# Tile 0 of the tokens in two column pieces, another load order, another order of the first W1 units, and the statistics of two tiles moved behind copies

## The chip, the cores and the metric

The kernel runs on one core of one Trainium2 chip. The metric is the device time of one execution in microseconds (us). A profile's "span" is the time from the first to the last instruction of the program in that one profiled execution; it is about 2 us less than the time of the same run. Engines: PE is the tensor engine, PEld its weight loads, DVE the vector engine, ACT the scalar engine, POOL the gpsimd engine, SP the engine that issues most loads.

Ratios are those of fast runs of one kernel over fast runs of the other in the same rounds, so they are not quite the ratio of the medians that are quoted beside them.

## The reference, cut to what matters

```python
xn = layernorm(x)                                   # x: 2048 tokens, 640 columns
out = x + attention(xn, wqkv, wo)                   # linear attention, 32 heads
        + gelu(xn @ w1 + b1) @ w2 + b2              # w1: 640 x 1536
```

The first matmul stage is `xn @ w1`. Before it a tile of 128 tokens has to be loaded, normalised, transposed (by PE) and copied from PSUM (the memory that PE's results go to) to SBUF (the memory that the next matmuls read). After all of W1 come the K stage (the matmuls for the keys) and, later, the q stage (those for the queries).

## The kernel before: the parts that matter

A helper records every instruction for an engine, and makes it wait for the writers of what it reads and the readers of what it overwrites. Each engine runs its own list in the order of the recording. The loads stand in one queue, issued by SP in this order:

```python
dma_x(0, 1)                                          # x tile 0
dma_w("sync", b1tmp[:], ..., r_b1tmp)                # bias, 3 KB
dma_w1(0)                                            # first quarter of W1: 384 of 1536 columns
dma_x(1, 1)
dma_w1(1)
dma_x(2, 1)
dma_w1(2)
dma_x(3, 1)
dma_w1(3)
# ... larger loads of x and the other weights follow
```

The helpers of one tile `t`:

```python
def ln_half(t, h):   # DVE: statistics of half of tile t's columns (needs x of the tile)
def ln_aggr(t):      # DVE: mean and variance; then two POOL instructions: rstd = 1 / sqrt(variance + eps)
def ln_norm(t):      # DVE: xn = (x - mean) * rstd, 640 columns
def transp(t):       # PE: five 128x128 transposes into a PSUM bank
def xnT_copy(t, b):  # DVE: PSUM -> SBUF, 640 columns
def b1_step():       # PE: transpose of the bias; ACT: copy of it
def h_unit(t0, n, jb):  # PE: 5 matmuls of n tiles with 128 columns of W1; ACT: gelu
```

The start and the order of the units, shortened: checks that a tile exists and the calls of `run_masks` (POOL work for a later stage) are left out (JT = 12 units of a tile, JQ = 3 units in each quarter of W1; `now` is the estimate of PE's time, in us):

```python
filler(11)                     # matmuls on zeros
ln_stats(0); ln_norm(0)
tb = transp(0)
b1_step()
filler(1)
ln_half(1, 0)
xnT_copy(0, tb)
ln_half(1, 1)
ln_aggr(1); ln_half(2, 0); ln_norm(1); ln_half(2, 1); ln_aggr(2)

plan = []
for q in range(2):
    plan += [(0, 1, jb) for jb in range(q * JQ, (q + 1) * JQ)]   # tile 0, quarters 0 and 1
for q in range(2):
    plan += [(1, 1, jb) for jb in range(q * JQ, (q + 1) * JQ)]   # tile 1, quarters 0 and 1
plan += [(0, 2, jb) for jb in range(2 * JQ, JT)]                 # both tiles, quarters 2 and 3
# ... then tile 2, tile 3, pairs, fours
now, nxt = 0.0, 1
for (t0, n, jb) in plan:
    while nxt < NT and (nxt < t0 + n or now >= 1.7 + 2.45 * (nxt - 1)):
        tb = transp(nxt)
        ln_half(nxt + 2, 0)        # statistics of a later tile ...
        xnT_copy(nxt, tb)          # ... ahead of the copy of this one
        ln_norm(nxt + 1)
        ln_half(nxt + 2, 1); ln_aggr(nxt + 2)
        nxt += 1; now += 0.3
    h_unit(t0, n, jb)
    now += 0.285 * n
```

Of the kernel before, what the change touches and what calls it, by code (L numbers as in the profile page):

```python
# [5 lines left out]
ALU = AluOpType  # L6
ACT = mybir.ActivationFunctionType
P = 128
FP32 = mybir.dt.float32
BF16 = mybir.dt.bfloat16  # L10
# [102 lines left out]
def bass_parallel_sum__linear_attn_block__dense_activation_gelu__prompt_kernel(  # L113
    nc: bass.Bass, A_x, A_wqkv, A_wo, B_x, B_w1, B_b1, B_w2, B_b2, out):
    Batch, S, D = A_x.shape
    F = B_w1.shape[1]
    assert Batch == 1 and D == 640 and F % P == 0 and S % 512 == 0
    NT = S // P
# [3 lines left out]
    DT = D // P  # L122
    JT = F // P
# [6 lines left out]
    Pl = Planner(nc)  # L130
    R_ = Pl.res
# [5 lines left out]
    with contextlib.ExitStack() as es:  # L137
# [3 lines left out]
        x_in = xPK  # L141
        PK = xPK
        xn_tm = sb("xn_tm", [P, NT, D], BF16)
        xnTf = sb("xnT", [P, DT * S], BF16)
        xnT = xnTf[:].rearrange("p (k s) -> p k s", k=DT)
        x_res = xnTf[:].rearrange("p (t d) -> p t d", t=NT)
        PQ = sb("PQ", [P, DT, S], BF16)
        HG = sb("HG", [P, JT, S], BF16)
        W1f = sb("W1", [P, DT * F], BF16)
        W1 = W1f[:].rearrange("p (k f) -> p k f", k=DT)  # L150
# [9 lines left out]
        b1tmp = sb("b1tmp", [JT, P], BF16)  # L160
        b1c = sb("b1c", [P, JT], FP32)
        b2bc = sb("b2bc", [P, D], BF16)
        ident = sb("ident", [P, P], BF16)
# [6 lines left out]
        aggr = sb("aggr", [P, 4, 2], FP32)  # L170
        veps = sb("veps", [P, 4], FP32)
        rstd = sb("rstd", [P, 4], FP32)
# [8 lines left out]
        B_ = [R_("bank%d" % i) for i in range(8)]  # L181
        ring = [0]

        def take(n):
            b = ring[0]
            if n == 2 and b % 2:
                b += 1
            b %= 8
            ring[0] = (b + n) % 8
            return b  # L190

        def bank(b, lo=0, hi=512):
            return ps[:, b * 512 + lo: b * 512 + hi]
# [7 lines left out]
        r_x = [R_("x%d" % t) for t in range(NT)]  # L201
        r_xr = [R_("xr%d" % c) for c in range(NC)]
        r_xb = [R_("xb%d" % t) for t in range(NT)]
        r_xn = [R_("xn%d" % t) for t in range(NT)]
        r_xnT = [R_("xnT%d" % t) for t in range(NT)]
        NW1 = 4
        r_W1 = [R_("W1_%d" % i) for i in range(NW1)]
        r_Wq, r_Wk, r_Wv, r_W2, r_Wo = R_("Wq"), R_("Wk"), R_("Wv"), R_("W2"), R_("Wo")
        r_b1tmp, r_b1c, r_b2 = R_("b1tmp"), R_("b1c"), R_("b2")
        r_ident, r_small, r_masks, r_bmask, r_warm = R_("ident"), R_("small"), R_("masks"), R_("bmask"), R_("warm")  # L210
        r_stats = [R_("stats%d" % i) for i in range(4)]
        r_aggr = [R_("aggr%d" % i) for i in range(4)]
        r_veps = [R_("veps%d" % i) for i in range(4)]
        r_rstd = [R_("rstd%d" % i) for i in range(4)]
# [3 lines left out]
        r_HG = [[R_("HG%d_%d" % (t, j)) for j in range(JT)] for t in range(NT)]  # L218
# [10 lines left out]
        def dma_x(t, n):  # L229
            src = xv[t * P:(t + n) * P, :].rearrange("(t p) d -> p t d", p=P)  # L230
            Pl.ins("sync", lambda e: e.dma_start(x_in[:, t:t + n, :], src),  # L231
                   writes=r_x[t:t + n], dma=True)

        def dma_w(eng, dst, src, res):
            Pl.ins(eng, lambda e: e.dma_start(dst, src), writes=[res], dma=True)  # L235
# [3 lines left out]
        FW = F // NW1  # L239
        def dma_w1(i):  # L240
            dma_w("sync", W1[:, :, i * FW:(i + 1) * FW], w1v[:, :, i * FW:(i + 1) * FW], r_W1[i])
        dma_x(0, 1)
        dma_w("sync", b1tmp[:], B_b1.rearrange("(a p) -> a p", p=P), r_b1tmp)
        dma_w1(0)
        dma_x(1, 1)
        dma_w1(1)
        dma_x(2, 1)
        dma_w1(2)
# [2 lines left out]
        for c in range(1, NC):  # L251
# [9 lines left out]
        v = "vector"  # L261
# [7 lines left out]
               reads=[r_ident], writes=[r_ident])  # L269
# [17 lines left out]
        def run_masks(n):  # L287
            for _ in range(min(n, len(mask_jobs))):
                mask_jobs.pop(0)()


        def filler(n):
            b = take(1)
            Pl.ins("tensor", [lambda e: e.matmul(bank(b), warm[:, 0:P], warm[:], start=True, stop=True)
                              for _ in range(n)], reads=[r_warm], writes=[B_[b]])

        def b1_step():
            b = take(1)
            Pl.ins("tensor", lambda e: e.transpose(bank(b).bitcast(BF16)[:, 0:JT], b1tmp[:], ident[:JT, :JT]),
                   reads=[r_b1tmp, r_ident], writes=[B_[b]])  # L300
            Pl.ins("scalar", lambda e: e.activation(b1c[:], bank(b).bitcast(BF16)[:, 0:JT], ACT.Copy),
                   reads=[B_[b]], writes=[r_b1c])


        def ln_half(t, h):
            s = t % 4
            Pl.ins(v, lambda e: e.bn_stats(stats[:, s, 6 * h:6 * h + 6], x_in[:, t, h * HW:(h + 1) * HW]),  # L307
                   reads=[r_x[t]], writes=[r_stats[s]])

        def ln_aggr(t):  # L310
            s = t % 4
            Pl.ins(v, lambda e: e.bn_aggr(aggr[:, s, :], stats[:, s, :]),
                   reads=[r_stats[s]], writes=[r_aggr[s]])
            Pl.ins(g, lambda e: e.tensor_single_scalar(veps[:, s:s + 1], aggr[:, s, 1:2], EPS, ALU.add),
                   reads=[r_aggr[s]], writes=[r_veps[s]])
            Pl.ins(g, lambda e: e.tensor_tensor(out=rstd[:, s:s + 1], in0=veps[:, s:s + 1],
                                                in1=mhalf[:], op=ALU.pow),
                   reads=[r_veps[s], r_small], writes=[r_rstd[s]])

        def ln_stats(t):  # L320
            ln_half(t, 0)
            ln_half(t, 1)
            ln_aggr(t)

        def ln_norm(t):
            s = t % 4
            Pl.ins(v, lambda e: e.tensor_scalar(xn_tm[:, t, :], x_in[:, t, :], aggr[:, s, 0:1], rstd[:, s:s + 1],
                                                ALU.subtract, ALU.mult),
                   reads=[r_x[t], r_aggr[s], r_rstd[s]], writes=[r_xn[t]])

        def transp(t):
            b = take(1)
            pT = bank(b).bitcast(BF16)[:, 0:D]
            Pl.ins("tensor", [(lambda e, k=k: e.transpose(pT[:, k * P:(k + 1) * P],  # L334
                                                          xn_tm[:, t, k * P:(k + 1) * P], ident[:]))
                              for k in range(DT)],
                   reads=[r_xn[t], r_ident], writes=[B_[b]])
            return b

        def xnT_copy(t, b):  # L340
            pT = bank(b).bitcast(BF16)[:, 0:D]
            Pl.ins(v, lambda e: e.tensor_copy(xnT[:, :, t * P:(t + 1) * P],  # L342
                                              pT.rearrange("p (k q) -> p k q", k=DT)),
                   reads=[B_[b]], writes=[r_xnT[t]])

        def h_unit(t0, n, jb):
# [8 lines left out]
                HG[:, jb, tok], bank(b, 0, w), ACT.Gelu_apprx_tanh, bias=b1c[:, jb:jb + 1]),  # L355
                reads=[B_[b], r_b1c], writes=[r_HG[t][jb] for t in range(t0, t0 + n)])

        Pl.ins("scalar", lambda e: e.activation(b1c[:, 0:1], warm[:, 0:1], ACT.Gelu_apprx_tanh),
               reads=[r_warm], writes=[r_b1c])
        filler(11)  # L360
        ln_stats(0)
        ln_norm(0)
        tb = transp(0)
        b1_step()
        filler(1)
        ln_half(1, 0)
        xnT_copy(0, tb)
        ln_half(1, 1)
        ln_aggr(1)
        ln_half(2, 0)  # L370
        ln_norm(1)
        ln_half(2, 1)
        ln_aggr(2)

        JQ = JT // NW1
        plan = []
        for q in range(2):
            plan += [(0, 1, jb) for jb in range(q * JQ, (q + 1) * JQ)]
        for q in range(2):
            plan += [(1, 1, jb) for jb in range(q * JQ, (q + 1) * JQ)]  # L380
        plan += [(0, 2, jb) for jb in range(2 * JQ, JT)]
        plan += [(2, 1, jb) for jb in range(JT)]
        plan += [(3, 1, jb) for jb in range(JT)]
        for (t0, n) in [(4, 2), (6, 2), (8, 4), (12, 4)]:
            plan += [(t0, n, jb) for jb in range(JT)]
        now, nxt = 0.0, 1
        for (t0, n, jb) in plan:
            while nxt < NT and (nxt < t0 + n or now >= 1.7 + 2.45 * (nxt - 1)):
                tb = transp(nxt)
                if nxt + 2 < NT:  # L390
                    ln_half(nxt + 2, 0)
                xnT_copy(nxt, tb)
                if nxt + 1 < NT:
                    ln_norm(nxt + 1)
                if nxt + 2 < NT:
                    ln_half(nxt + 2, 1)
                    ln_aggr(nxt + 2)
                    run_masks(2)
                nxt += 1
                now += 0.3  # L400
            h_unit(t0, n, jb)
            now += 0.285 * n
# [19 lines left out]
        for t in range(NT):  # L422
            b = take(2)
# [11 lines left out]
        for f in range(DT):  # L435
            b = take(2)
            for t in range(NT):
# [3 lines left out]
                    reads=[r_xn[t], r_PK[t]], writes=B_[b:b + 2])  # L441
            Pl.ins("scalar", lambda e, b=b, f=f: e.activation(halves(GTb[:, f, :]), pair(b), ACT.Copy),
                   reads=B_[b:b + 2], writes=[r_GT[f]] + r_W1)

        Pl.ins(v, lambda e: e.tensor_tensor(out=zsum, in0=PK[:, 0, :], in1=PK[:, 1, :], op=ALU.add),
               reads=[r_PK[0], r_PK[1]], writes=[r_zsum])
        for t in range(2, NT):
            Pl.ins(v, lambda e, t=t: e.tensor_tensor(out=zsum, in0=zsum, in1=PK[:, t, :], op=ALU.add),
                   reads=[r_PK[t], r_zsum], writes=[r_zsum])
# [3 lines left out]
               reads=[r_zsum, r_zhl], writes=[r_zhl])  # L453
# [162 lines left out]
```

## Time and profile before

| | before |
|---|---|
| median of 4 runs | 220.77 us (220.66 to 221.13) |
| span of the profile | 218.7 us |
| PE busy | 210.3 us, 96% |
| first W1 matmul | 7.26 us |
| PE without a gap from | 11.10 us |
| x3 landed | 10.13 us |
| third quarter of W1 landed | 9.66 us |

The head of the profile's page says which engine is full (busy us, share of the span, instructions):

```profile
span 218.7 us, 4004 instructions
PE 210.3 (96%) x1633; PEld 144.8 (66%) x1642; DVE 125.6 (57%) x227; ACT 74.3 (34%) x140; POOL 41.8 (19%) x74
```

The chain of waits goes back from the last instruction, at each step to what released it. Columns: start in us, length in us, what. Its part in the first 14 us:

```profile
4.21 5.92 DMA xPK<-in_A_x_dram
10.13 0.02 issue
10.16 0.49 DVE stats L307
10.65 0.40 DVE xnT L342
11.05 0.05 issue
11.10 2.40 PE ps L350 x35
```

From 11.10 us on, the chain is PE up to 109 us, but for a few issue gaps of 0.05 us. So time saved ahead of 11.10 us reaches the end. The chain reads: x3 lands at 10.13, the statistics of tile 3 are taken (L307), only then is tile 1 copied (L342), and only then does PE go on (L350). But tile 1 has no need of x3. The timeline shows the same stretch with the engines side by side (start, length, engine, line, operation, out<-in, shape, count; in brackets the idle time of the engine before it and what ended it):

```profile
7.26 1.83 PE L350 MATMUL ps<-xnT,W 128*128 128x128 bf16 x30 [0.44 <-DVE xnT L342]
9.34 0.45 PE L334 MATMUL ps<-ident,xn_tm 128*128 128x128 bf16 x5 [0.24 <-DVE xn_tm L327]
10.16 0.49 DVE L307 BATCH_NORM_STATS2 stats<-xPK 128x6 f32<-128x320 bf16 x1 [0.23 <-DMA xPK<-in_A_x_dram]
10.57 0.47 DVE L342 COPY xnT<-ps 128x640 bf16<-128x640 bf16 x1
11.10 2.40 PE L350 MATMUL ps<-xnT,W 128*128 128x128 bf16 x35 [1.30 <-DVE xnT L342]
```

The transposes of tile 1 (L334) were through at 9.79 us, and the copy came at 10.57. The engine runs its list in order, and the statistics stood first. PE stood 1.30 us.

### The profile page before, as it was taken

The page shows a single profiled execution, that of the slowest core. Times are in us where ns is not written, and L with a number is a line of the kernel's source. Part 1 is how long each engine was busy: PE and PEld are TensorE (multiplying, and loading weights), DVE is VectorE, ACT ScalarE, POOL GpSimd, SP SyncE. Part 2 cuts the span into 40 slices and gives each one's busy share as a digit, 9 for nine tenths or more (in the row PEclk, how much of TensorE's full clock was granted, in tenths as well). Part 3 has the DMA queues.
Part 4 walks back from the last instruction along what each step waited for, and adds up shares of the span by engine and source line. Part 5 has one row for each costly group of instructions (what it writes and reads, how often), then busy time and mean ns, then how long its engine had stood idle before and what let it go on. Part 6 is the DMA issues. An engine that isn't in the chain of part 4 may idle for free.

```text
span 218.7 us, 4004 instructions
## 1 busy us (share of the span) xinstructions
PE 210.3 (96%) x1633; PEld 144.8 (66%) x1642; DVE 125.6 (57%) x227; ACT 74.3 (34%) x140; POOL 41.8 (19%) x74
## 2 busy tenths in 40 slices
PE   7699999999999999999999799999999999999994
PEld 2499999544447777777756555667767776777773
DVE  2767778600004888899268769869939315712211
ACT  2378877566667555211153652500000000000000
POOL 2236555200000000000000000079994000000000
PEclk9999999999999999999999999999999999999999
DMA  5999970000000000000000000334420010010011
GB/s 158 339 363 365 361 256 0 1 3 0 0 0 0 3 0 3 0 0 0 3 0 1 0 3 0 118 125 124 153 86 30 35 58 30 24 39 30 30 52 42
DMA packets 13706, 15.50 MB, mean 71 GB/s; under 512 B 632, under 2 KB 13688, under 8 KB 13688
## 3 DMA queue, kind: packets, MB, share of 16 engines
q1 hardware_dynamic: 13688, 15.24, 21.2%
q8 instruction: 13, 0.21, 0.4%
q14 instruction: 5, 0.04, 0.1%
HBM read 12.62 MB, written 2.62 MB: 70 GB/s over the span
## 4 chain that ended last, share of the span: by engine, by line
PE 82%; DVE 11%; DMA 3%; SPq 1%; issue 1%; ACT 0%; DVEq 0%
PE ps L551 34%; PE ps L350 23%; PE ps L438 10%; PE ps L427 10%; DVE PQ L417 5%; DMA xPK<-in_A_x_dram 3%; PE ps L507 2%; PE ps L334 2%; DVE ek L415 2%; DVE rden L512 2%; DVE PQ L514 1%; SPq L235 1%; DVE W L484 1%; SPq L231 1%; DVE ZB L474 1%
## 5 line engine op out<-in xcount | busy, mean ns | idle before, releaser
L350 PE MATMUL ps<-xnT,W 128*128 128x128 bf16 (+2 forms) x447 | 54.8, 279 | 1.9 <-DVE xnT L342 1.7
L551 PE MATMUL ps<-W,HG 128*128 128x320 bf16 x384 | 54.9, 299 | 0.2 <-DVE PQ L417 0.2
L551 PEld LDWEIGHTS ps<-W,HG 128*128 128x128 bf16 x384 | 37.5, 98 | 15.7 <-issue 0.7
L354 ACT ACTIVATE HG<-ps,b1c 128x128 bf16<-128x128 f32 (+2 forms) x90 | 41.1, 489 | 18.8 <-PE ps L350 17.3
L350 PEld LDWEIGHTS ps<-xnT,W 128*128 128x128 bf16 x450 | 36.0, 98 | 16.9 <-DVE xnT L342 1.5
L523 POOL TENSOR_TENSOR xnT<-xnT,b2bc 128x640 bf16<-128x640 bf16 x16 | 22.6, 1452 | 100.7 <-DMA xnT<-in_A_x_dram 100.7
L557 DVE TENSOR_TENSOR out_sb<-ps,xnT 128x640 bf16<-128x640 f32 x15 | 12.2, 821 | 33.5 <-PE ps L551 30.6
L414 ACT ACTIVATE ek<-ps 128x512 bf16<-128x512 f32 (+1 forms) x36 | 23.2, 645 | 23.6 <-PE ps L427 9.2
L415 DVE TENSOR_SCALAR ek<-ek 128x512 bf16<-128x512 bf16 (+1 forms) x36 | 10.9, 303 | 30.7 <-ACT ek L414 29.5
L551 PE MATMUL ps<-Msb,PQ 128*128 128x320 bf16 x160 | 24.5, 299 | 0.0
L427 PE MATMUL ps<-Wqkv,xnT 128*128 128x320 bf16 x160 | 21.9, 299 | 0.0
L438 PE MATMUL ps<-xPK,xn_tm 128*128 128x320 bf16 x160 | 21.9, 299 | 0.0
L460 PE MATMUL ps<-xnT,Wqkv 128*128 128x512 bf16 x97 | 21.6, 379 | 0.2
L427 PEld LDWEIGHTS ps<-Wqkv,xnT 128*128 128x128 bf16 x160 | 15.7, 98 | 6.2
L551 PEld LDWEIGHTS ps<-Msb,PQ 128*128 128x128 bf16 x160 | 15.7, 98 | 6.1
L438 PEld LDWEIGHTS ps<-xPK,xn_tm 128*128 128x128 bf16 x160 | 15.7, 98 | 6.1
L460 PEld LDWEIGHTS ps<-xnT,Wqkv 128*128 128x128 bf16 x100 | 11.7, 117 | 9.5
L307 DVE BATCH_NORM_STATS2 stats<-xPK 128x6 f32<-128x320 bf16 x32 | 15.1, 471 | 4.4 <-DMA xPK<-in_A_x_dram 4.3
L417 DVE SCALAR_TENSOR_TENSOR PQ<-ps,ek 128x512 bf16<-128x512 f32 x20 | 13.8, 691 | 2.1
L417 DVE SCALAR_TENSOR_TENSOR xPK<-ps,ek 128x640 bf16<-128x640 f32 x16 | 13.2, 824 | 1.7
L512 DVE RECIPROCAL rden<-den_sb 128x512 bf16<-128x512 f32 x4 | 13.4, 3353 | 0.1
L514 DVE TENSOR_TENSOR PQ<-PQ,rden 128x512 bf16<-128x512 bf16 x20 | 12.2, 673 | 0.1
(50 smaller groups left out, 105.5 us busy)
## 6 DMA issues: line engine op xcount, KB each, us to landing
xnT<-in_A_x_dram SPq DMA_DIRECT2D x4, 640.0 KB, 4.4
Wqkv<-in_A_wqkv_dram SPq DMA_DIRECT2D x3, 800.0 KB, 12.1
out_dram<-out_sb SPq DMA_DIRECT2D x15, 160.0 KB, 1.8
W<-in_B_w_dram SPq DMA_DIRECT2D x4, 480.0 KB, 5.5
xPK<-in_A_x_dram SPq DMA_DIRECT2D x3, 640.0 KB, 8.7
W<-in_B_w_dram SPq DMA_DIRECT2D x1, 1920.0 KB, 14.5
Wo<-in_A_wo_dram SPq DMA_DIRECT2D x1, 800.0 KB, 9.8
xPK<-in_A_x_dram SPq DMA_DIRECT2D x4, 160.0 KB, 4.5
```

Source lines behind the costliest of these rows:

```text
L307: Pl.ins(v, lambda e: e.bn_stats(stats[:, s, 6 * h:6 * h + 6], x_in[:, t, h * HW:(h + 1) * HW]), reads=[r_x[t]], writes=[r_stats[s]])
L350: Pl.ins("tensor", [(lambda e, k=k: e.matmul(bank(b, 0, w), W1[:, k, jb * P:(jb + 1) * P], xnT[:, k, tok], start=(k == 0), stop=(k == DT - ...
L354: Pl.ins("scalar", lambda e: e.activation(HG[:, jb, tok], bank(b, 0, w), ACT.Gelu_apprx_tanh, bias=b1c[:, jb:jb + 1]), reads=[B_[b], r_b1c ...
L414: Pl.ins("scalar", lambda e: e.activation(e2, src, ACT.Exp), reads=br, writes=[r_ek[s]])
L415: Pl.ins(v, lambda e: e.tensor_scalar(et, et, 1.0, 1e-6, ALU.min, ALU.add), reads=[r_ek[s]], writes=[r_ek[s]])
L417: Pl.ins(v, lambda e: e.scalar_tensor_tensor(out=d2, in0=src, scalar=0.0, in1=e2, op0=ALU.max, op1=ALU.add), reads=br + [r_ek[s]], writes= ...
L427: fns.append(lambda e, k=k, h=h, b=b, t=t: e.matmul(bank(b + h, 0, HW), xnT[:, k, t * P:(t + 1) * P], Wqkv[:, k, D + h * HW:D + (h + 1) * ...
L438: Pl.ins("tensor", [(lambda e, t=t, h=h, b=b, f=f: e.matmul(bank(b + h, 0, HW), xn_tm[:, t, f * P:(f + 1) * P], PK[:, t, h * HW:(h + 1) * ...
L460: Pl.ins("tensor", [(lambda e, k=k, j=j, b=b: e.matmul(bank(b), Wqkv[:, k, j:D:DT], xnT[:, k, cc], start=(k == 0), stop=(k == DT - 1))) fo ...
L512: Pl.ins(v, lambda e: e.reciprocal(rden[:], den_sb[:]), reads=[r_den], writes=[r_rden])
L523: Pl.ins(g, lambda e: e.tensor_tensor(out=x_res[:, t, :], in0=x_res[:, t, :], in1=b2bc[:], op=ALU.add), reads=[r_xr[t // CH], r_b2], write ...
L551: return lambda e: e.matmul(bank(b + h, 0, HW), seq[i][0], seq[i][1][:, h * HW:(h + 1) * HW], start=(i == 0), stop=(i == n - 1))
```

## The change

Its intent is to start W1 earlier and to keep PE fed. Tile 0 is normalised, transposed and copied in two column pieces, so that the first matmuls start on the first piece. x1 is second in the load queue, and the bias goes to ACT's queue. Three quarters of W1 instead of two are used for tiles 0 and 1 singly; the last is used for both together. The statistics of tiles 3 and 4 go behind the copies of tiles 1 and 2.

```diff
         dma_x(0, 1)
-        dma_w("sync", b1tmp[:], B_b1.rearrange("(a p) -> a p", p=P), r_b1tmp)
+        dma_x(1, 1)
         dma_w1(0)
-        dma_x(1, 1)
         dma_w1(1)
 ...
+        dma_w("scalar", b1tmp[:], B_b1.rearrange("(a p) -> a p", p=P), r_b1tmp)
-        filler(11)
+        filler(10)
         ln_stats(0)
-        ln_norm(0)
-        tb = transp(0)
+        ln_half(1, 0)
+        ln_half(1, 1)
+        norm0(0, CA, r_xnA)                    # CA = 256 columns
+        norm0(CA, D, r_xnB)                    # the other 384
+        dA, sA, bA = transp0(0, 2, r_xnA)
+        filler(1)
+        dB, sB, bB = transp0(2, DT, r_xnB)
+        Pl.ins(v, lambda e: e.tensor_copy(dA, sA), ...)
+        Pl.ins("scalar", lambda e: e.activation(dB, sB, ACT.Copy), ...)
         b1_step()
-        filler(1)
-        ln_half(1, 0)
-        xnT_copy(0, tb)
-        ln_half(1, 1)
         ln_aggr(1)
 ...
+        h_first([0, 1, 2])                     # units 0 to 2: first k = 0, 1, then k = 2, 3, 4
-        for q in range(2):
-            plan += [(0, 1, jb) for jb in range(q * JQ, (q + 1) * JQ)]
-        for q in range(2):
-            plan += [(1, 1, jb) for jb in range(q * JQ, (q + 1) * JQ)]
-        plan += [(0, 2, jb) for jb in range(2 * JQ, JT)]
+        plan = [(0, 1, jb) for jb in range(3, 3 * JQ)]
+        plan += [(1, 1, jb) for jb in range(3 * JQ)]
+        plan += [(0, 2, jb) for jb in range(3 * JQ, JT)]
 ...
-        now, nxt = 0.0, 1
+        now, nxt = 0.7, 1
-            while nxt < NT and (nxt < t0 + n or now >= 1.7 + 2.45 * (nxt - 1)):
+            while nxt < NT and (nxt < t0 + n or now >= 2.0 + 2.45 * (nxt - 1)):
                 tb = transp(nxt)
-                if nxt + 2 < NT:
+                early = nxt > 2 and nxt + 2 < NT
+                if early:
                     ln_half(nxt + 2, 0)
                 xnT_copy(nxt, tb)
 ...
+                    if not early:
+                        ln_half(nxt + 2, 0)
                     ln_half(nxt + 2, 1)
```

With the new plan the transposes of tile 1 fall behind unit 7 of tile 0, and units 6 to 8 need the third quarter of W1.

More of the change, by code (lines that the diff above doesn't have):

```diff
@@ L356, in h_unit, with norm0, transp0 @@
                 reads=[B_[b], r_b1c], writes=[r_HG[t][jb] for t in range(t0, t0 + n)])
+        CA = 2 * P
+        r_xnA, r_xnB = R_("xn0A"), R_("xn0B")
+        def norm0(lo, hi, res):
+            Pl.ins(v, lambda e: e.tensor_scalar(xn_tm[:, 0, lo:hi], x_in[:, 0, lo:hi], aggr[:, 0, 0:1], rstd[:, 0:1],
+                                                ALU.subtract, ALU.mult),
+                   reads=[r_x[0], r_aggr[0], r_rstd[0]], writes=[res, r_xn[0]])
+        def transp0(k0, k1, res):
+            b = take(1)
+            pT = bank(b).bitcast(BF16)
+            Pl.ins("tensor", [(lambda e, k=k: e.transpose(pT[:, (k - k0) * P:(k - k0 + 1) * P],
+                                                          xn_tm[:, 0, k * P:(k + 1) * P], ident[:]))
+                              for k in range(k0, k1)],
+                   reads=[res, r_ident], writes=[B_[b]])
+            return xnT[:, k0:k1, 0:P], pT[:, 0:(k1 - k0) * P].rearrange("p (k q) -> p k q", k=k1 - k0), b
@@ new lines, in h_first @@
+        def h_first(jbs):
+            bs = [take(1) for _ in jbs]
+            for (ks, res) in (((0, 1), r_xnTA), ((2, 3, 4), r_xnT[0])):
+                for jb, b in zip(jbs, bs):
+                    Pl.ins("tensor", [(lambda e, k=k, jb=jb, b=b: e.matmul(
+                        bank(b, 0, P), W1[:, k, jb * P:(jb + 1) * P], xnT[:, k, 0:P],
+                        start=(k == 0), stop=(k == DT - 1))) for k in ks],
+                        reads=[r_W1[jb * P // FW], res], writes=[B_[b]])
+            for jb, b in zip(jbs, bs):
+                Pl.ins("scalar", lambda e, jb=jb, b=b: e.activation(
+                    HG[:, jb, 0:P], bank(b, 0, P), ACT.Gelu_apprx_tanh, bias=b1c[:, jb:jb + 1]),
+                    reads=[B_[b], r_b1c], writes=[r_HG[0][jb]])
@@ L358, in bass_parallel_sum__linear_attn_block__dense_activation_gelu__prompt_kernel @@
+        r_xnTA = R_("xnT0A")
         Pl.ins("scalar", lambda e: e.activation(b1c[:, 0:1], warm[:, 0:1], ACT.Gelu_apprx_tanh),
                reads=[r_warm], writes=[r_b1c])
-        filler(11)
+        dma_w("scalar", b1tmp[:], B_b1.rearrange("(a p) -> a p", p=P), r_b1tmp)
+        filler(10)
         ln_stats(0)
-        ln_norm(0)
-        tb = transp(0)
+        ln_half(1, 0)
[3 more added lines that the diff above has]
+        dA, sA, bA = transp0(0, 2, r_xnA)
@@ L364, in bass_parallel_sum__linear_attn_block__dense_activation_gelu__prompt_kernel @@
+        filler(1)
+        dB, sB, bB = transp0(2, DT, r_xnB)
+        Pl.ins(v, lambda e: e.tensor_copy(dA, sA), reads=[B_[bA]], writes=[r_xnTA])
+        Pl.ins("scalar", lambda e: e.activation(dB, sB, ACT.Copy), reads=[B_[bB]], writes=[r_xnT[0]])
         b1_step()
-        filler(1)
-        ln_half(1, 0)
-        xnT_copy(0, tb)
-        ln_half(1, 1)
         ln_aggr(1)
@@ L373, in bass_parallel_sum__linear_attn_block__dense_activation_gelu__prompt_kernel @@
         ln_aggr(2)
+        h_first([0, 1, 2])
         JQ = JT // NW1
-        plan = []
-        for q in range(2):
-            plan += [(0, 1, jb) for jb in range(q * JQ, (q + 1) * JQ)]
-        for q in range(2):
-            plan += [(1, 1, jb) for jb in range(q * JQ, (q + 1) * JQ)]
-        plan += [(0, 2, jb) for jb in range(2 * JQ, JT)]
+        plan = [(0, 1, jb) for jb in range(3, 3 * JQ)]
+        plan += [(1, 1, jb) for jb in range(3 * JQ)]
+        plan += [(0, 2, jb) for jb in range(3 * JQ, JT)]
         plan += [(2, 1, jb) for jb in range(JT)]
```

## The prediction

> **What bounds the kernel.** The tensor engine: PE is busy 210.3 us of a 218.7 us span (page), and the chain of waits is unbroken PE work from 11.10 to 109.33 us, a PE/DVE mix to 138 us (q stage), then PE to the end. The change touches only the first 45 us or so, and what lies between there and 109 us is PE, so a saving at the start should arrive at the end whole. There is only PE's idle time before 11.10 us to be had. By the timeline PE starts the first W1 matmuls at 7.26 us; in the window 7.26 to 11.10 it is busy 2.29 of 3.84 us. Most of the rest is one wait of 1.30 us before 11.10: the tile-1 copy (DVE, 10.57) stood behind the statistics of tile 3, which waited for x3 (landed 10.13), though tile 1's transposes began at 9.34.
>
> **What the change does.**
> 1. Statistics of tile 3 move behind that copy: the wait for x3 goes.
> 2. x1 is issued near 1.2 us instead of 2.14 and should land near 3.6 instead of 6.21. Its two statistics (0.49 us each) fit in the DVE's 1.08 us wait for tile 0's rstd.
> 3. Tile 0 in pieces. Normalising 640 columns took 0.45 us; my estimate for 256 and 384 is 0.25 and 0.31. Transposes A start about 5.75, copy A (DVE, estimate 0.25) ends about 6.3, copy B (ACT; 640 columns took 0.70, 12 took 0.18, so about 0.49) about 6.9. W1 matmuls start about 6.35, and three units are finished at about 7.45 instead of 8.1.
> 4. But units 6 and 7 of tile 0 now precede tile 1's transposes, and need the third quarter of W1. It landed at 9.66 us; with x1 in the slack at the queue's start I expect 9.2 to 9.6. PE ends unit 5 at about 8.3 to 8.6 and then stands about 0.9 us, which gives up point 3's head start.
> 5. Then units 6, 7 (0.55), transposes (0.28) and the copy (0.47 with latencies, unit 8 beneath it): tile 1's matmuls start at about 10.8 to 11.2, with nine units of tile 0 done instead of six. The extra three are worth 0.83 us, the start 0 to 0.3. Thereafter PE should run without a gap: the last quarter (landed 11.63) isn't needed before about 13.5.
>
> Filler, bias load on ACT's queue (landing about 5 us, needed at 6.2) and the added instructions are off the path. The Trainium skill, "TensorE: Matmul & The Clock Gate", section "Why this matters for your kernels", warns of idle gaps over about 3 us; gaps near 1 us should keep the clock. In this trace filler weight loads come every 0.43 us until 5.06 us.
>
> **Prediction.** About 1.0 us saved: 219.75 us, 219.0 to 220.5 eight times in ten. Faster by over 2%: 0.01; within 2%: 0.98; slower by over 2%: 0.01.
>
> **What would show it.** x1 landing before 4.4 us; no wait for x3 ahead of the tile-1 copy; copies A and B ending near 6.3 and 6.9; a PE gap of about 0.9 us ending with the third quarter of W1; tile 1's matmuls at about 11.0; PE unbroken afterwards; q and output stages as long as before, only earlier.
>
> **What would make it wrong.** The third quarter landing after 9.7 us (only about 0.5 saved); x1 after 4.4 us, blocking tile 0's normalisation; the bias after 6.3 us, blocking PE; the clock rising later, as only ten fillers precede the first transposes.

## The result, and the profile after

| | before | after |
|---|---|---|
| median | 220.77 us (220.66 to 221.13, 4 runs) | 220.26 us (219.97 to 220.57, 4 runs) |
| ratio | | 0.9975, 95% interval 0.9955 to 0.9994 |
| span of the profile | 218.7 us | 218.0 us |
| first matmul of the K stage (behind all W1 units) | 65.70 us | 64.96 us |

The interval lies just below 1. The profile is of the fastest of the four runs (span 218.0 us; the others 218.2 to 218.6), so what it shows as gained is at the upper end. The head of the page after:

```profile
span 218.0 us, 4045 instructions
PE 210.7 (97%) x1656; PEld 144.9 (66%) x1656; DVE 126.0 (58%) x228; ACT 75.3 (35%) x144; POOL 41.7 (19%) x74
```

The same part of the chain of waits, after (L349 is now the W1 matmul, L333 the transposes, L341 the copy):

```profile
3.30 6.25 DMA W<-in_B_w_dram
9.55 0.05 issue
9.60 0.73 PE ps L349 x10
10.33 0.29 PE ps L333 x5
10.62 0.02 issue
10.64 0.50 DVE xnT L341
11.15 0.05 issue
11.19 2.13 PE ps L349 x35
```

A load is still the root of the chain, but another one: the third quarter of W1, landed at 9.55 us, instead of x3. The timeline after:

```profile
6.44 0.49 ACT L402 ACTIVATE xnT<-ps 128x384 bf16<-128x384 bf16 x1 [4.15 <-PE ps L369]
6.44 1.22 PE L379 MATMUL ps<-xnT,W 128*128 128x128 bf16 x15
7.61 1.01 PE L349 MATMUL ps<-xnT,W 128*128 128x128 bf16 x15
9.60 0.73 PE L349 MATMUL ps<-xnT,W 128*128 128x128 bf16 x10 [0.98 <-DMA W<-in_B_w_dram]
10.16 0.44 PE L333 MATMUL ps<-ident,xn_tm 128*128 128x128 bf16 x5
10.64 0.49 DVE L341 COPY xnT<-ps 128x640 bf16<-128x640 bf16 x1 [1.09 <-PE ps L333]
11.19 2.13 PE L349 MATMUL ps<-xnT,W 128*128 128x128 bf16 x35 [0.31 <-DVE xnT L341]
```

PE starts W1 0.82 us earlier (6.44 instead of 7.26). It then stands 0.98 us for the load and 0.31 us for the copy. Tile 1's matmuls start at 11.19 us, 0.09 us later than before. The gain is that nine units of tile 0 are done by then instead of six: three units, 0.83 us. That makes 0.83 - 0.09 = 0.74 us, and the K stage starts just 0.74 us earlier (64.96 against 65.70). Nothing is lost or won after that: from the K stage's first matmul to the end it takes 153.02 us before and 153.00 us after.

So the arithmetic of the one pair of traces closes. But it does not say which part of the change did it, or where the early start went. The theories:

- A: the gain is the wait for x3, taken off tile 1's copy by the moved statistics. All else cancels out.
- B: the gain comes from tile 0 in pieces and the early x1.
- C: in the changed kernel the landing of the third quarter of W1 sets the time. Every other part could be undone without loss, and the early start is swallowed by that wait.

### The profile page after: what moved, and what is told of

Its sections match the earlier page's. It is cut to its first block, busy times and chain, and to the rows that moved or that the text cites. A ratio compares the mean times of both kernels' runs of the same rounds, so it can differ in the third digit from the quotient of the medians.

```text
span 218.0 us, 4045 instructions
## 1 busy us (share of the span) xinstructions
PE 210.7 (97%) x1656; PEld 144.9 (66%) x1656; DVE 126.0 (58%) x228; ACT 75.3 (35%) x144; POOL 41.7 (19%) x74
## 4 chain that ended last, share of the span: by engine, by line
PE 82%; DVE 11%; DMA 3%; issue 1%; SPq 1%; ACT 0%; DVEq 0%
PE ps L587 34%; PE ps L349 23%; PE ps L463 10%; PE ps L474 10%; DVE PQ L453 5%; DMA W<-in_B_w_dram 3%; PE ps L543 2%; PE ps L333 2%; DVE ek L451 2%; DVE rden L548 2%; DVE PQ L550 1%; DVE W L520 1%; SPq L231 1%; DVE ZB L510 1%; PE ps L532 1%
## 5 line engine op out<-in xcount | busy, mean ns | idle before, releaser
L349 PE MATMUL ps<-xnT,W 128*128 128x128 bf16 (+2 forms) x450 | 54.5, 278 | 1.3 <-DMA W<-in_B_w_dram 1.0
L349 PEld LDWEIGHTS ps<-xnT,W 128*128 128x128 bf16 x450 | 35.5, 98 | 16.3 <-DMA W<-in_B_w_dram 1.1
L496 PE MATMUL ps<-xnT,Wqkv 128*128 128x512 bf16 x100 | 22.1, 379 | 0.0
L341 DVE COPY xnT<-ps 128x640 bf16<-128x640 bf16 x15 | 7.4, 492 | 9.0 <-PE ps L333 8.8
```

What stands on the lines that cost most here:

```text
L349: Pl.ins("tensor", [(lambda e, k=k: e.matmul(bank(b, 0, w), W1[:, k, jb * P:(jb + 1) * P], xnT[:, k, tok], start=(k == 0), stop=(k == DT - ...
L496: Pl.ins("tensor", [(lambda e, k=k, j=j, b=b: e.matmul(bank(b), Wqkv[:, k, j:D:DT], xnT[:, k, cc], start=(k == 0), stop=(k == DT - 1))) fo ...
```

## The experiments

Each kernel ran five rounds beside the kernel before on the same chip, in four groups. The medians:

| run | median, us (range, runs) | before, same rounds | ratio, 95% interval |
|---|---|---|---|
| e0_changed_again | 220.18 (219.96 to 221.16, 6) | 220.85 | 0.9970 (0.9934 to 1.0006) |
| e1_stats_behind_copy | 220.22 (219.96 to 220.82, 6) | 220.85 | 0.9963 (0.9929 to 0.9996) |
| e2_stats_ahead_again | 219.97 (219.73 to 220.52, 6) | 220.85 | 0.9950 (0.9916 to 0.9984) |
| e3_tile0_whole | 220.17 (219.72 to 220.39, 6) | 220.85 | 0.9956 (0.9923 to 0.9989) |
| e4_tile1_first | 219.11 (218.93 to 219.49, 6) | 220.74 | 0.9921 (0.9896 to 0.9947) |
| e5_plan_only | 220.00 (219.75 to 220.39, 6) | 220.74 | 0.9957 (0.9934 to 0.9981) |
| e6_x1_third | 220.10 (219.70 to 220.20, 6) | 220.74 | 0.9957 (0.9934 to 0.9980) |
| e8_tile1_first_x1_third | 219.93 (219.79 to 220.00, 6) | 220.74 | 0.9952 (0.9930 to 0.9975) |
| e7_tile1_first_whole | 218.95 (218.89 to 219.44, 5) | 221.06 | 0.9888 (0.9844 to 0.9931) |
| e4b_tile1_first_again | 218.97 (218.81 to 219.20, 4) | 221.06 | 0.9884 (0.9841 to 0.9928) |
| e9_third_quarter_later | 220.78 (220.57 to 222.05, 6) | 221.06 | 0.9981 (0.9940 to 1.0022) |
| e10_whole_early_rstd | 218.72 (218.46 to 219.05, 5) | 221.18 | 0.9889 (0.9871 to 0.9906) |

Some runs of before (up to 223.05 us) and of e9 had a granted clock of 0.991 or 0.992 and were 1.3 us or more above the median of the others in their rounds. They pull the means. So the medians and the traces are the better guide between experiments. Where two runs of different groups are compared, their distance from before in their own rounds is the fairer measure.

### e1: the moved statistics alone, on the kernel before

```diff
                 tb = transp(nxt)
-                if nxt + 2 < NT:
+                early = nxt > 2 and nxt + 2 < NT
+                if early:
                     ln_half(nxt + 2, 0)
                 xnT_copy(nxt, tb)
 ...
+                    if not early:
+                        ln_half(nxt + 2, 0)
                     ln_half(nxt + 2, 1)
```

> The kernel before with one part of the change: the statistics of tiles 3 and 4 go behind the copy and the normalisation of tiles 1 and 2. Theory A (the measured gain is the wait for x3 taken off the tile-1 copy, all else cancels out): the copy of tile 1 starts about 9.95 us instead of 10.57, tile 1's matmuls about 10.5 instead of 11.10, and the time falls by 0.5 to 0.6 us, as much as the whole change gained. Theory B (the gain comes from tile 0 in pieces and the early x1): the time stays within 0.2 us of before.

Measured: 220.22 us against 220.85 of before, as much as the whole change in the same rounds (220.18). The timeline of e1:

```profile
9.40 0.45 PE L334 MATMUL ps<-ident,xn_tm 128*128 128x128 bf16 x5 [0.24 <-DVE xn_tm L327]
9.91 0.48 DVE L342 COPY xnT<-ps 128x640 bf16<-128x640 bf16 x1
10.44 2.40 PE L350 MATMUL ps<-xnT,W 128*128 128x128 bf16 x35 [0.59 <-DVE xnT L342]
```

The copy follows the transposes at once, and tile 1's matmuls start at 10.44 us instead of 11.10. The K stage starts at 65.05 us. x3 landed at 10.39 us in this run, and nothing waited for it any more. These lines of the diff alone are worth the whole measured gain when they are put on the kernel before. Theory B is not needed for the gain.

### e2: the same lines undone in the changed kernel

```diff
-                early = nxt > 2 and nxt + 2 < NT
+                early = nxt + 2 < NT
```

> The changed kernel with the statistics of tiles 3 and 4 ahead of the copy again, as before. Theory A as first put (this part carries the gain in the changed kernel also): 0.5 us slower than the changed kernel. Theory C (in the changed kernel tile 1's transposes wait for the third quarter of W1, which lands within 0.5 us of x3, so this part no longer matters there): within 0.15 us of the changed kernel.

Measured: 219.97 us against 220.18 of the changed kernel, so certainly not slower. Theory A as first put falls: the lines that carry the gain on the kernel before carry nothing in the changed one. The timeline of e2 shows why:

```profile
9.72 0.73 PE L349 MATMUL ps<-xnT,W 128*128 128x128 bf16 x10 [0.97 <-DMA W<-in_B_w_dram]
10.15 0.49 DVE L306 BATCH_NORM_STATS2 stats<-xPK 128x6 f32<-128x320 bf16 x1 [0.47 <-DMA xPK<-in_A_x_dram]
10.29 0.44 PE L333 MATMUL ps<-ident,xn_tm 128*128 128x128 bf16 x5
10.77 0.49 DVE L341 COPY xnT<-ps 128x640 bf16<-128x640 bf16 x1
```

The statistics of tile 3 are ahead of the copy again and wait for x3. But they are done at 10.64 us, while the transposes, held up by the third quarter of W1, end at 10.73.

### e3: tile 0 whole again in the changed kernel

```diff
-        norm0(0, CA, r_xnA)
-        norm0(CA, D, r_xnB)
-        ... transposes, filler and copies in pieces ...
-        b1_step()
+        ln_norm(0)
+        tb = transp(0)
+        b1_step()
+        filler(1)
+        xnT_copy(0, tb)
 ...
-        h_first([0, 1, 2])
+        for jb in range(3):
+            h_unit(0, 1, jb)
```

> The changed kernel with tile 0 normalised, transposed and copied whole again (one 640-column instruction each, copy on DVE). Theory A/C (the pieces are absorbed by the 0.98 us wait of PE for the third quarter of W1): same time as the changed kernel within 0.15 us, and the wait shorter by what the start is later. Theory B: 0.4 to 0.6 us slower. By the durations of the trace the first three units would end near 7.6 us, not later than in pieces, as the ACT copy of piece B takes as long as the DVE copy of the whole.

Measured: 220.17 us against 220.18. The pieces bring nothing here. The timeline of e3:

```profile
6.90 1.83 PE L349 MATMUL ps<-xnT,W 128*128 128x128 bf16 x30 [0.24 <-DVE aggr L311]
9.65 0.73 PE L349 MATMUL ps<-xnT,W 128*128 128x128 bf16 x10 [0.92 <-DMA W<-in_B_w_dram]
```

W1 starts at 6.90 us, 0.46 us after the first piece in the changed kernel, and PE still stands 0.92 us for the third quarter. (The line names the aggregation of tile 1 as what W1 waited for; the matmuls read the copy of tile 0, through at 6.75 us, and nothing of that aggregation.) Even without the late wait little was there to be had. After the 15 matmuls of three units the 16th starts at 7.73 us. In pieces the last nine of the 15 start at 6.98 (the weight loads behind the ACT copy), so they end near 7.5, and the next unit waited for the second quarter of W1, landed at 7.56. Most of the 0.6 us that the prediction gave to the pieces came from elsewhere: before, tile 0's copy stood behind a half of tile 1's statistics, which waited for x1 (landed 6.21). All profiles together say it more sharply. The 15th W1 matmul starts at 8.04 and 8.10 us in before and e1, at 7.67 to 7.84 us with the whole tile and the statistics out of the way (e3, e7, e10; mean 7.76), and at 7.44 to 7.92 us in pieces (nine profiles; mean 7.71).

### e0: the changed kernel again

> The changed kernel itself, for a ratio on the same chip and rounds and a second look at when the third quarter of W1 lands. If the landing sets its time, the time follows it: about 218.0 us of span at a landing of 9.55 us, later by as much as the landing is later. Expected ratio to before 0.9975, within 0.9965 and 0.9985.

Measured: 220.18 us against 220.85, ratio 0.9970. The third quarter landed at 9.88 us, 0.33 later than in the first profile, and the K stage started at 65.30 us, 0.34 later. The wait is the same:

```profile
9.93 0.73 PE L349 MATMUL ps<-xnT,W 128*128 128x128 bf16 x10 [0.97 <-DMA W<-in_B_w_dram]
```

### e9: the third quarter of W1 landing later

```diff
-        dma_w1(2)
         dma_x(3, 1)
+        dma_w1(2)
         dma_w1(3)
```

> The changed kernel with the third quarter of W1 behind x3 in the load queue, so that it lands later by one x tile, about 0.45 us (near 10.0 to 10.3 us). In the runs of the changed kernel and of e2, e3 and e6 the K stage starts 55.41 us after that landing. If the landing sets the time: it again starts 55.4 us after it, and the time is 0.4 to 0.5 us above the changed kernel, close to before. If not: the time stays within 0.15 us of the changed kernel.

Measured: 220.78 us, 0.6 above the changed kernel (e0, another group). Against before in the same rounds the gain falls from 0.67 us (e0) to 0.28 us; the intervals of the two ratios overlap, so the traces have to carry this point. The third quarter landed at 10.38 us, and the wait grew from 0.98 us:

```profile
10.43 0.73 PE L349 MATMUL ps<-xnT,W 128*128 128x128 bf16 x10 [1.43 <-DMA W<-in_B_w_dram]
```

The table sets the landing in the trace against the first matmul of the K stage, for the changed kernel and all experiments that keep its order of units:

| profile | third quarter landed, us | K stage starts, us | difference |
|---|---|---|---|
| e6 | 9.44 | 64.85 | 55.41 |
| after | 9.55 | 64.96 | 55.41 |
| e3 | 9.61 | 65.02 | 55.41 |
| e2 | 9.67 | 65.09 | 55.42 |
| e0 | 9.88 | 65.30 | 55.42 |
| e9 | 10.38 | 65.79 | 55.41 |

Over a range of 0.94 us in the landing the difference stays within 0.01 us, whichever part was undone. Theory C is shown for the start of the K stage: with this order of units the landing of the third quarter of W1 sets it, and none of the three parts that were undone singly (e2, e3, e6) matters. The bias load and the filler were not undone, nor were several parts at once.

### e6: x1 third in the load queue again

```diff
-        dma_x(1, 1)
         dma_w1(0)
+        dma_x(1, 1)
 ...
-        ln_half(1, 0)
-        ln_half(1, 1)
         norm0(0, CA, r_xnA)
 ...
         b1_step()
+        ln_half(1, 0)
+        ln_half(1, 1)
         ln_aggr(1)
```

> The changed kernel with x1 behind the first quarter of W1 in the load queue again, and its statistics behind tile 0's copy. x1 lands near 6.2 us and tile 1 is normalised near 9.2, still before the transposes at 10.16. Theory C: within 0.15 us of the changed kernel (0.9955 to 0.998 of before). If the early x1 carries gain: 0.4 us slower or more.

Measured: 220.10 us, ratio 0.9957. The place of x1 brings nothing in the changed kernel. Nor can it be seen to move the third quarter. With x1 second that landed at 9.55 to 10.05 us in nine profiles (mean 9.76); with x1 third at 9.44 to 9.90 in four (before, e1, e6, e8; mean 9.72). The same loads are ahead of it in both orders.

### e5: the order of units alone put back

```diff
-        plan = [(0, 1, jb) for jb in range(3, 3 * JQ)]
-        plan += [(1, 1, jb) for jb in range(3 * JQ)]
-        plan += [(0, 2, jb) for jb in range(3 * JQ, JT)]
+        plan = [(0, 1, jb) for jb in range(3, 2 * JQ)]
+        plan += [(1, 1, jb) for jb in range(2 * JQ)]
+        plan += [(0, 2, jb) for jb in range(2 * JQ, JT)]
```

> The changed kernel with the order of units alone put back (two quarters of W1 before the shared ones, tile 1's transposes after unit 5); the vector engine's order stays. The wait for the third quarter goes, but the copy of tile 1 stands behind the statistics of tile 2, which wait for x2 (landed 8.05): the copy ends near 10.1 us and tile 1's matmuls start near 10.15 with six units done. Expected 0.2 us below the changed kernel. If instead the order of units were the whole loss: 1 us below or more.

Measured: 220.00 us, 0.18 below the changed kernel of another group; against before in their own rounds the gains are 0.74 and 0.67 us, so no difference is shown. The wait for the third quarter is gone, and the next one takes its place. The timeline of e5:

```profile
8.56 0.49 DVE L306 BATCH_NORM_STATS2 stats<-xPK 128x6 f32<-128x320 bf16 x1 [1.99 <-DMA xPK<-in_A_x_dram]
8.97 0.43 DVE L326 TENSOR_SCALAR xn_tm<-xPK,aggr,rstd 128x640 bf16<-128x640 bf16 x1
9.97 0.48 DVE L341 COPY xnT<-ps 128x640 bf16<-128x640 bf16 x1
10.50 2.94 PE L349 MATMUL ps<-xnT,W 128*128 128x128 bf16 x40 [0.59 <-DVE xnT L341]
```

DVE stands 1.99 us for x2 (landed 8.54), with tile 1's normalisation behind it in its list, though tile 1 needs only x1. It is the same fault as in the kernel before, one tile earlier. So the order of units is not the whole loss.

### e4: tile 1 ahead of the statistics of tile 2, and the old order of units

Several statements are put on one line here.

```diff
         ln_aggr(1)
-        ln_half(2, 0)
         ln_norm(1)
-        ln_half(2, 1)
-        ln_aggr(2)
         h_first([0, 1, 2])
 ... plan as in e5 ...
-            while nxt < NT and (nxt < t0 + n or now >= 2.0 + 2.45 * (nxt - 1)):
+            while nxt < NT and (nxt < t0 + n or
+                                now >= {1: 0.95, 2: 5.0}.get(nxt, 2.0 + 2.45 * (nxt - 1))):
                 tb = transp(nxt)
+                if nxt == 1:
+                    xnT_copy(1, tb)
+                    ln_half(2, 0); ln_half(2, 1); ln_aggr(2)
+                    ln_half(3, 0); ln_half(3, 1)
+                    ln_norm(2); ln_aggr(3)
+                    run_masks(2)
+                    nxt += 1; now += 0.3
+                    continue
```

> The changed kernel with tile 1 ready before the third quarter of W1 is needed: the normalisation and the copy of tile 1 go ahead of the statistics of tile 2, tile 1's transposes stand after unit 3 of tile 0, and only the first two quarters of W1 are used before both tiles can share the rest. If the changed kernel gives its gain back to the wait for the third quarter of W1 (theory C), PE no longer stands 0.98 us for it: tile 1's matmuls start near 8.9 us with six units done, the K stage starts near 63.5 us instead of 64.96, and the time falls to about 218.7 us, 1.5 below the changed kernel, and no longer follows the landing of that quarter. Rival (PE is held by the loads as a whole, so that another load takes over the wait): less than 0.5 us gained, with a PE wait for another DMA in the trace.

Measured: 219.11 us, and 218.97 in the repeat; before had 220.74 and 221.06 in the same rounds. It beats both kernels. The timeline of e4:

```profile
7.61 0.45 DVE L326 TENSOR_SCALAR xn_tm<-xPK,aggr,rstd 128x640 bf16<-128x640 bf16 x1 [1.08 <-POOL rstd L315]
8.12 0.45 PE L333 MATMUL ps<-ident,xn_tm 128*128 128x128 bf16 x5
8.41 4.24 PE L349 MATMUL ps<-xnT,W 128*128 128x128 bf16 x55
8.61 0.49 DVE L341 COPY xnT<-ps 128x640 bf16<-128x640 bf16 x1 [0.55 <-PE ps L333]
9.16 3.21 PEld L349 LDWEIGHTS ps<-xnT,W 128*128 128x128 bf16 x45 [0.20 <-DVE xnT L341]
```

Tile 1's matmuls start at 9.16 us (expected: 8.9), and the longest waits of PE behind the first three units are 0.2 us. The third quarter of W1 landed at 9.75 us and is first needed about 10.8, so nothing waits for it. The K stage starts at 63.73 us, 1.23 earlier than in the first profile of the changed kernel. The time fell by less than expected (218.7), in part because the stretch from the K stage on took 0.3 us more in this profile (below). The rival, that PE is held by the loads as a whole, falls. The views by stretch of the same 3.84 us put it in one figure (columns: stretch, length, busy us of PE, PEld, DVE, ACT and POOL with instructions, clock, DMA share, GB/s); first before, then after, then e4:

```profile
7.26:11.10 3.84, 2.29 (x35) 1.95 (x36) 2.96 (x9) 1.76 (x6) 1.59 (x4) 1.00 1.09 335
```

```profile
7.26:11.10 3.84, 2.65 (x43) 2.19 (x40) 1.91 (x6) 2.48 (x9) 0.87 (x3) 1.00 1.09 347
```

```profile
7.26:11.10 3.84, 3.81 (x62) 3.43 (x61) 2.83 (x7) 3.26 (x12) 0.90 (x3) 1.00 1.09 341
```

The loads run at the same rate in all three (335 to 347 GB/s). Only in e4 is PE busy through the stretch.

### e8: e4 with x1 third in the queue

The edit is that of e6, on the kernel of e4.

> The kernel of e4_tile1_first with x1 behind the first quarter of W1 again. Here nothing else hides x1: its statistics start near 6.3 us, rstd comes near 8.4, the copy of tile 1 ends near 9.9, so tile 1's matmuls start near 9.95 instead of 8.9: about 1.0 us slower than e4_tile1_first. If x1's place does not matter there either: within 0.2 us of it.

Measured: 219.93 us, 0.82 slower than e4. The timeline of e8:

```profile
8.79 0.45 DVE L326 TENSOR_SCALAR xn_tm<-xPK,aggr,rstd 128x640 bf16<-128x640 bf16 x1 [1.07 <-POOL rstd L315]
9.30 0.45 PE L333 MATMUL ps<-ident,xn_tm 128*128 128x128 bf16 x5 [0.88 <-DVE xn_tm L326]
```

Tile 1's normalisation starts 1.18 us later than in e4, and PE stands 0.88 us for it. The early x1 is worth about 0.8 us, but only once tile 1 is not held up by something else. In the changed kernel that worth was there and could not be seen.

### e7 and e4b: e4 with tile 0 whole, and e4 again

The edit of e7 is that of e3, on the kernel of e4.

> The kernel of e4_tile1_first with tile 0 whole again (as in e3_tile0_whole). There the wait for the third quarter of W1 is gone, so nothing late hides the pieces. Theory D (the pieces bring nothing in any case, since the second quarter of W1 lands only at 7.5 to 7.8 us, about when three units are done either way): within 0.2 us of e4_tile1_first. Rival (the pieces are worth their head start once the late wait is gone): 0.4 to 0.6 us slower.

> The kernel of e4_tile1_first again, as the partner of e7_tile1_first_whole on the same chip and rounds, and a second look at its stages: 0.992 of before, tile 1's matmuls near 9.1 us, no PE wait over 0.3 us after 7.8 us.

Measured: 218.95 and 218.97 us. In time the pieces show no worth. The traces differ, though: the K stage starts at 64.16 us in e7, and at 63.73 and 63.81 in the two profiles of e4, because in e7 the normalisation of tile 1 started at 8.05 us instead of 7.61. Its aggregation stood behind a copy of 640 columns. From the K stage to the end e7 then took 152.95 us, and e4 153.27 and 153.29, so that both end at the same time. I can't call theory D (the pieces bring nothing in any case) shown by these runs.

### e10: tile 0 whole, and the aggregation of tile 1 ahead of the copy

The edit is shown against e7.

```diff
         ln_norm(0)
+        ln_aggr(1)
         tb = transp(0)
         b1_step()
         filler(1)
         xnT_copy(0, tb)
-        ln_aggr(1)
         ln_norm(1)
```

> The kernel of e7_tile1_first_whole (tile 0 whole, tile 1 first) with one more instruction moved: the aggregation of tile 1's statistics goes into the vector engine's 0.55 us wait ahead of the copy of tile 0. In e7 tile 1's normalisation started at 8.05 us, 0.43 later than in e4 with the pieces, as the aggregation stood behind the longer copy. If that was all that the pieces were worth there, the normalisation now starts near 7.0 us, tile 1's matmuls near 9.0, and the K stage near 63.6 us instead of 64.16, without pieces. The time is then 218.6 to 219.0 us, as the q stage was 0.3 us longer in both profiles of e4 than in e7. If the pieces have a worth of their own: the K stage not before 63.9 us.

Measured: 218.72 us against 221.18 of before, the lowest median of all. The timeline of e10:

```profile
7.07 0.45 DVE L326 TENSOR_SCALAR xn_tm<-xPK,aggr,rstd 128x640 bf16<-128x640 bf16 x1 [0.16 <-POOL rstd L315]
8.09 0.28 PEld L349 LDWEIGHTS ps<-xnT,W 128*128 128x128 bf16 x5 [0.21 <-DMA W<-in_B_w_dram]
```

The normalisation starts at 7.07 us, as expected, but the K stage came at 63.98 us, later than the 63.9 that I had set as the mark. By the letter this is for a worth of the pieces. But in this run the second quarter of W1 landed at 8.05 us, against 7.78 and 7.82 in e4, and PE waited for it. Measured from that landing the K stage starts after 55.93 us in e10, and after 55.95 and 56.00 us in e4. So PE goes on from the second quarter in the same way with and without the pieces. By the matmuls' starts PE was ready for the fourth unit near 7.89 us in e10 and began it at 7.83 us in e4, so with e4's landing the whole tile would have cost about 0.06 us (an estimate from these starts). That is how I read it; with one profile of e10 it is well supported, not shown. The kernel without pieces is simpler and no slower.

### What stays open

The stretch from the K stage to the end takes 152.95 to 153.03 us in ten profiles and 153.27 to 153.29 in four (e3, e4, e4b, e6). The traces tell where the 0.3 us arise: in each of the four, DVE stands once for 0.46 to 0.48 us between its five products with `maskKV` in the q stage, 52.6 to 53.4 us after the K stage's start; in the ten others it stands there 0.19 us at most. What causes it was not looked for. And why the loads land up to 0.6 us later in one run than in another was not settled.

## Why the prediction was right, point by point

The time (220.26 us) lies in the range, and "within 2%" is what came. The gain was forecast as 1.0 us. It was 0.51 us between the medians of the first job, 0.67 in e0's rounds and 0.74 at the K stage of the first pair of traces. So the mechanism held for the gap and its end, and the size was half to three quarters of what I gave. The range was wide, 0.3 to 1.8 us saved, and the result lies in its smaller part: that the time fell inside says less than the traces do. The prediction's own list of what would make it wrong had a third quarter that lands after 9.7 us, with only about 0.5 us saved; e0 has just that (9.88 us, and 0.40 us at the K stage).

1. "The wait for x3 goes." It went, and e1 shows that this alone is worth the whole measured gain on the kernel before. What I did not see: by e2 it is not needed in the changed kernel, where tile 1's transposes come so late that x3 is there anyway. I listed it as a contribution of the changed kernel, and it is none.
2. "x1 should land near 3.6": 3.99 us in that profile, 3.58 in e0. It fitted in the wait for rstd. By e6 it is worth nothing in the changed kernel; by e8 about 0.8 us where tile 1 comes first.
3. Tile 0 in pieces: W1 at 6.44 us (forecast 6.35), copies ended 6.26 and 6.93 (6.3 and 6.9), three units near 7.5 (7.45). The times were right for this profile, the earliest of nine with pieces. But the 0.6 us head start was credited to the pieces, and by e3 the whole tile starts W1 at 6.90 us, against 7.26 before: most of it came from the statistics of tile 1, moved from between transposes and copy.
4. The wait for the third quarter of W1: forecast about 0.9 us, measured 0.98 in the first profile of the changed kernel and 0.97 in e0. That the head start is given up there is what e2, e3, e6 and the table under e9 show.
5. Tile 1's matmuls "start at about 10.8 to 11.2": 11.19 and, in e0, 11.53 us. This is the term that was mis-sized. I expected the third quarter to land up to 0.46 us earlier than 9.66 as x1 would fill slack at the start of the queue, and counted 0 to 0.3 us for it. It landed at 9.55 and 9.88 us. Over all profiles the place of x1 does not move it (means 9.76 and 9.72 us), and the first quarter gave way: it landed at 5.48 to 6.68 us with x1 ahead of it (ten profiles), at 5.23 to 5.96 with x1 behind (four). So of 0.83 + (0 to 0.3) us only the 0.83 for three units came, less 0.09 us (first profile) or 0.43 us (e0) for the later start: 0.74 and 0.40 us, which is what the K stage's start shows (64.96 and 65.30 us against 65.70).

The Trainium skill's "TensorE: Matmul & The Clock Gate", section "Why this matters for your kernels", which warns of idle gaps over about 3 us, was rightly used: after the 0.98 us gap ten matmuls of 128 columns started at 9.60 us and the transposes behind them at 10.16, 56 ns for each matmul, the same as later. No run here has a gap of 3 us between matmuls, so the limit itself was not tested.

## What to carry to other kernels

An engine's list is a queue. An instruction that waits for a load holds up all behind it, so the order should be that in which the inputs land, with the work that the bottleneck needs next in front; e4, with that order, gained 1.6 and 2.1 us on before, the change 0.5 and 0.7. When a head start is bought, look for the next load on the path: what comes before it is worth nothing until the work that does not need that load is put ahead of it. And undo the parts one at a time: here each of three could be taken out of the changed kernel without loss, though one of them, alone, gave all of the gain and another was worth 0.8 us in a better order.

## What the Trainium skill lacked or had wrong

- "DMA: Bandwidth & Descriptors", section "Why a DMA increments its semaphore by 16 and not by 1", says that up to 16 DMA engines finish independently. The load of the third quarter has 16 marks, from 8.69 to 9.55 us, but the page has no figure for the spread. For the second and third quarters of W1 it was 0.64 to 0.66 us in the profile of before, and 0.83 to 1.79 us in the 13 others. Once up, it stayed much the same from load to load within a run (e5: 1.68 to 1.79 us over eight loads on end), so that a lag of one engine, or a few, would move every landing behind it; that this is the cause was not shown.
- "TensorE: Matmul & The Clock Gate", section "Back-to-back issue gap", gives some 81 ns (128 columns) and 131 ns (512 columns) as the sustained spacing of matmuls that each load new weights. Here 35 matmuls of 128 columns took 1.95 us of the chain, 56 ns each, and 95 of 512 columns took 20.50 us, 216 ns each (both in the profile after). These are the figures that the page gives for isolated matmuls.
- The same page, "Part 4: PE-mode transpose", gives a transpose of 128x128 as about 275 ns in a kernel. The trace gives single ones 219 ns, with ends that the profile models; five in a row took 0.28 us of the chain, 56 ns each. The page lacks the figure for a row of them.
- The same page, "Part 1: The HAM clock gate", puts the rise of the clock at about 4 us into matmul activity, with 0.5 us either way, and calls it run-variable. With matmuls from 1.24 us on, the clock records of the 14 profiles turn to full at 3.94 us (e2) to 7.16 us (e9), 2.7 to 5.9 us after the first matmul: a wider range. The filler between the pieces of tile 0 took 0.38 us in the first profile of the changed kernel and 0.63 us in e5, where the rise came late (6.71 us).
- No page has it: on one core, 7 of the 118 runs (5 of before, 2 of e9) had a mean granted clock of 0.991 or 0.992 and took 222.01 to 223.05 us, where the same kernels otherwise took 220.4 to 221.8. Their cause was not sought.
